# A new order for the first loads and early work, and one product moved between two attention bursts

## The chip, the cores and the metric

The kernel runs on one core of a Trainium2 chip. The metric is the device time of one execution in microseconds (us), the median of the runs. Five queues of instructions run beside one another and meet only at semaphores: TensorE (PE: matmuls, with the weight loads shown apart as PEld), VectorE (DVE), ScalarE (ACT), GpSimd (POOL) and SyncE (SP, which here issues nearly all DMAs).

## The reference

Four layers with residual connections on a sequence of S = 2048 tokens of width D = 448 in bf16: local attention (A), a gated feed-forward (B), A again and B again. Both attention layers use the same weights, and so do both feed-forward layers.

```python
def _A_ref(x, wqkv, wo):                 # H = 16 heads of 28, W, dil = 8, 2
    qkv = (x @ wqkv).reshape(B, S, 3, H, Dh)        # q, k, v by head
    # token t sees the keys t, t-2, ..., t-14
    logits = einsum("bhsd,bhswd->bhsw", q, kg) * Dh ** -0.5
    attn = softmax(where(mask, logits, -1e9))
    return einsum("bhsw,bhswd->bhsd", attn, vg).reshape(B, S, D) @ wo

def _B_ref(x, w_gate, w_up, w_down):     # F = 1792
    return ((x @ w_gate) * (x @ w_up)) @ w_down

x = x + _A_ref(_layernorm(x), A_wqkv, A_wo)
x = x + _B_ref(_layernorm(x), B_w_gate, B_w_up, B_w_down)
x = x + _A_ref(_layernorm(x), A_wqkv, A_wo)
x = x + _B_ref(_layernorm(x), B_w_gate, B_w_up, B_w_down)
```

## The kernel before

x stays in SBUF as 16 blocks of 128 tokens. In the code the layers are numbered 0 to 3; 0 and 2 are attention, so "the second layer" of attention is layer 2. The attention layers are cut into chunks of tokens: layer 0 into 256, 512, 512, 512 and 256, that is blocks 0-1, 2-5, 6-9, 10-13 and 14-15.

Work is first described as some 1580 numbered operations, each with the engines it may run on and what it depends on. No planner decides on the order: the table `ORDER` (line 103) lists by hand, for each of the five engines, the numbers of its operations in the order of execution, and so also says which of ACT and DVE makes a copy that either could make. The table `BANKS` (line 164) gives for each operation of PE that opens accumulators the PSUM banks (of eight) that it takes. A bank must have been read by its last user before it is taken again; `schedule` (line 223) derives that wait from the two tables, and `emit` (line 273) writes the instructions and semaphore waits out. An instruction at the head of an engine's queue that waits holds up all that stand behind it.

The head of the kernel, up to about 50 us, is what most of the change touches:

- SP issues the loads of x (line 443, called from `load_x`, line 448) in six pieces: operation 0 is block 0, 1 is block 1, 2 is blocks 2-3, 7 is blocks 4-7, 12 is blocks 8-11, 13 is blocks 12-15. Operations 3 to 6 load four pieces of the Q/K weight into a staging area (3 is piece 1, 4 is piece 3, 5 is piece 0, 6 is piece 2), 8 and 9 the V weight, 72 to 83 the gate and up weights, 84 to 87 the output weight `wo_g`, 71 writes constant rows of ones to a scratch tensor in DRAM that V passes through later.
- Layer norm of a block: DVE takes statistics (lines 571 and 573), ACT turns the variance into 1/std with two small functions (574, 576), DVE normalises into `xn_sb` (592). PE transposes the block (602 for the first two blocks, 606 for others), and ACT or DVE copies the result into `xnTa` (613, 616).
- ACT and DVE copy the staged Q/K weight into its padded form `WQK`, in eight pieces (line 510); later DVE adds small extra columns (518).
- PE makes V of a group of query blocks (`v_group`, copies at 766 to 793) and Q and K of a chunk (`qk_chunk`): four groups of fourteen matmuls each, 256 or 512 columns wide. All ordinary matmuls come from one helper and have line 351. A pair of matmuls on the two halves of the array's rows runs side by side. ACT or DVE copies a group to `qk` (701).
- Attention of a group of query blocks: DVE makes two masked copies of Q (`Qz`, 812), PE the scores (S, line 826), ACT the exponential (835), DVE the mask (842), PE the product with V (AV, line 860: 64 small matmuls in a burst), ACT and DVE copy it to `O_sb` (871, 875), and a normalisation follows (DVE 885, ACT 886 and 887, DVE 898). The output projection (`y_blocks`, PE line 351 with `wo_g`) adds to x at 915.

A large product is "crossed": its two accumulators are each fed from both halves of the rows, first one way, then the other. The second half of the work waits for the first (line 639), and each half may itself be two operations. For the down projection of a feed-forward chunk (`twin_blocks`, line 656, called with line 977) that makes four operations of fourteen matmuls: 1240, 1241, 1242 and 1243 for blocks 4 and 5 in layer 3, each 448 columns wide. Operation 1233 is to blocks 2 and 3 what 1241 is to 4 and 5.

In the second attention layer PE has 1308, the AV burst of group 6, directly followed by 1330, the AV burst of group 7, and then 1241. Elsewhere in PE's list an entry such as `1303*1.3.5/1223` mixes a burst into another operation's matmuls.

Of the kernel before, what the change touches and what calls it, by code (L numbers as in the profile page):

```python
# [95 lines left out]
def grp_nc(g):  # L96
# [35 lines left out]
    ),  # L132
    "dve": (
# [46 lines left out]
)  # L180


class Op:
    __slots__ = ("engs", "ins", "est", "deps", "mode", "prio", "acquire", "release", "idx", "eng",
                 "dma", "after", "selfd", "alt")

    def __init__(self, **kw):
        for k in self.__slots__:
            setattr(self, k, kw.get(k))
# [907 lines left out]
```

## Time and profile before

| | us |
|---|---|
| median of 3 runs | 383.92 (383.89 to 384.61) |
| the profiled execution | 384.08 |
| its span, first to last instruction | 382.3 |
| PE busy | 376.2 |
| DVE busy | 286.4 |
| ACT busy | 205.1 |

In the rows below, a line of the timeline reads: start, duration, engine, source line, operation, the tile written and the tiles read, shape, how many instructions were merged into the row, and in brackets the idle time in front and what ended it. A line of the waits reads: who waited for whom, us in total, times, and the longest. "issue" stands for waiting that nothing in the profile explains. In the chain, a row has its start, duration and what ran. The granted clock (PEclk) is in tenths of full speed, cut off at 9.

### The profile page before, as it was taken

What the parts mean: (1) busy time and instruction counts of PE and PEld (TensorE: products, weight loads), DVE (VectorE), ACT (ScalarE), POOL (GpSimd) and SP (SyncE); (2) the same over time, 40 slices, a digit from 0 to 9 for tenths busy, and PEclk for the clock granted to TensorE, in tenths of its full rate; (3) what the DMA queues carried; (4) which work ended last, traced back from release to release, by engine and by line L of the source; (5) the groups of instructions that cost most, each with busy time, mean ns of one, the idle gap of its engine ahead of it and who ended that gap; (6) DMA issues with size and microseconds to landing.
All of it is one profiled execution on the core that took longest, in us unless ns stands there. A gap on an engine that the chain in (4) does not pass through costs nothing.

```text
span 382.3 us, 14251 instructions
## 1 busy us (share of the span) xinstructions
PE 376.2 (98%) x6322; PEld 210.1 (55%) x6322; DVE 286.4 (75%) x643; ACT 205.1 (54%) x390; POOL 5.0 (1%) x25
## 2 busy tenths in 40 slices
PE   8999999999999999999999999999999999999997
PEld 3545587544445445444756765545555444446664
DVE  7987999998976786787677985637998698455323
ACT  4999886756426552564465525547744635133320
POOL 5000000000000000000000000000000000000000
PEclk9999999999999999999999999999999999999999
DMA  7756633610611033031101135320125004140003
GB/s 241 195 139 174 91 90 102 84 23 2 89 35 38 2 60 62 15 67 26 32 14 33 20 43 101 39 45 4 27 34 74 3 2 68 32 115 30 3 2 98
DMA packets 54881, 22.50 MB, mean 59 GB/s; under 512 B 45012, under 2 KB 54820, under 8 KB 54820
## 3 DMA queue, kind: packets, MB, share of 16 engines
q1 hardware_dynamic: 54676, 21.53, 27.8%
q8 instruction: 50, 0.82, 0.9%
q14 instruction: 11, 0.09, 0.1%
q10 hardware_dynamic: 144, 0.06, 0.1%
HBM read 8.54 MB, written 2.71 MB: 29 GB/s over the span
## 4 chain that ended last, share of the span: by engine, by line
PE 92%; ACT 2%; DVE 2%; DMA 1%; SPq 1%; issue 1%; DVEq 0%
PE ps L351 83%; PE ps L354 3%; PE ps L860 2%; PE ps L826 2%; PE ps L966 1%; DMA hT<-in_A_wqkv_dram 1%; ACT qk L701 1%; SPq L443 1%; ACT E_sb L835 1%; DVE xn_sb L592 0%; PE ps L606 0%; ACT xnTa L616 0%; DVE Qz L812 0%; DVE R_sb L885 0%; ACT lnv L574 0%
## 5 line engine op out<-in xcount | busy, mean ns | idle before, releaser
L351 PE MATMUL ps<-xnTb,WGU 64*128 64x512 bf16 (+1 forms) x1894 | 172.4, 332 | 0.0
L351 PEld LDWEIGHTS ps<-xnTb,WGU 64*128 64x128 bf16 x1894 | 92.0, 94 | 69.8 <-issue 1.4
L951 ACT ACTIVATE g_sb<-ps 128x512 bf16<-128x512 f32 (+1 forms) x140 | 70.1, 510 | 85.0 <-PE ps L351 65.2
L954 DVE TENSOR_TENSOR hT<-g_sb,ps 128x512 bf16<-128x512 bf16 (+1 forms) x140 | 78.2, 575 | 47.0 <-ACT g_sb L951 44.5
L351 PE MATMUL ps<-WD,hT 64*128 64x448 bf16 x812 | 82.8, 350 | 0.0
L351 PEld LDWEIGHTS ps<-WD,hT 64*128 64x128 bf16 x812 | 38.8, 94 | 34.8 <-DVE hT L954 0.3
L351 PE MATMUL ps<-xnTa,WQK 64*128 64x512 bf16 (+1 forms) x494 | 53.3, 353 | 0.3 <-DVE WQK L518 0.2
L915 DVE TENSOR_TENSOR x_sb<-x_sb,ps 128x448 bf16<-128x448 bf16 x62 | 37.2, 613 | 15.6 <-PE ps L351 15.3
L835 ACT ACTIVATE E_sb<-ps,shift_sb 128x1024 bf16<-128x1024 f32 (+1 forms) x36 | 37.1, 1068 | 12.7 <-PE ps L826 12.5
L571 DVE BATCH_NORM_STATS2 st<-x_sb 128x6 f32<-128x448 bf16 x64 | 38.8, 616 | 1.6 <-DMA x_sb<-in_A_x_dram 1.1
L592 DVE TENSOR_SCALAR xn_sb<-x_sb,mv,rstd 128x512 bf16<-128x512 bf16 (+1 forms) x64 | 35.4, 567 | 5.5 <-ACT rstd L576 5.5
L351 PEld LDWEIGHTS ps<-xnTa,WQK 64*128 64x128 bf16 x494 | 23.2, 94 | 21.5 <-ACT E_sb L835 0.5
L701 ACT ACTIVATE qk<-ps 128x1024 bf16<-128x1024 f32 (+1 forms) x29 | 27.0, 950 | 14.3 <-PE ps L351 14.2
L351 PE MATMUL ps<-wo_g,oT 64*128 64x448 bf16 x250 | 28.7, 350 | 0.0
L842 DVE TENSOR_TENSOR E_sb<-E_sb,MK 128x1024 bf16<-128x1024 bf16 (+1 forms) x36 | 23.3, 659 | 5.3 <-ACT E_sb L835 5.2
L886 ACT ACTIVATE R_sb<-R_sb 128x480 f32<-128x480 f32 (+1 forms) x34 | 20.3, 602 | 10.8 <-DVE R_sb L885 10.8
L898 DVE TENSOR_TENSOR oT<-O_sb,R_sb 128x480 bf16<-128x480 f32 (+3 forms) x36 | 22.1, 624 | 4.3 <-ACT R_sb L887 4.2
L351 PE MATMUL ps<-WV,xnTa 64*128 64x336 bf16 (+3 forms) x252 | 24.0, 305 | 0.1
L885 DVE STREAM_SHUFFLE R_sb<-O_sb 128x480 f32<-128x480 f32 (+1 forms) x34 | 23.1, 694 | 0.0
L574 ACT ACTIVATE lnv<-mv,eps_sb 128x2 f32<-128x2 f32 (+1 forms) x33 | 9.4, 294 | 22.3 <-DVE mv L573 22.2
L887 ACT ACTIVATE R_sb<-R_sb 128x480 f32<-128x480 f32 (+1 forms) x34 | 20.2, 602 | 0.6
L871 ACT ACTIVATE O_sb<-ps 128x512 f32<-128x512 f32 (+3 forms) x19 | 10.3, 557 | 14.1 <-PE ps L860 14.1
(60 smaller groups left out, 214.1 us busy)
## 6 DMA issues: line engine op xcount, KB each, us to landing
out_dram<-x_sb SPq DMA_DIRECT2D x15, 112.0 KB, 1.8
x_sb<-in_A_x_dram SPq DMA_DIRECT2D x3, 448.0 KB, 6.6
hT<-in_A_wqkv_dram SPq DMA_DIRECT2D x4, 224.0 KB, 5.1
WGU<-in_B_w_gate_dram SPq DMA_DIRECT2D x4, 224.0 KB, 3.5
WGU<-in_B_w_up_dram SPq DMA_DIRECT2D x4, 224.0 KB, 3.5
WD<-in_B_w_down_dram SPq DMA_DIRECT2D x2, 448.0 KB, 3.8
WGU<-in_B_w_gate_dram SPq DMA_DIRECT2D x2, 336.0 KB, 4.7
WGU<-in_B_w_up_dram SPq DMA_DIRECT2D x2, 336.0 KB, 4.9
```

The lines of the kernel that those rows point to most:

```text
L351: return lambda E: E.matmul(out(), lhs(), rhs(), start=start, stop=stop)
L571: sc.add("dve", one(lambda E, B=B: E.bn_stats(st6[:, B, :], x_sb[:, B, :]), ("bn", li, B)), 525.0, deps=[("x", li - 1, B)] + ([("xn", li - ...
L592: sc.add("dve", one(lambda E, B=B, dst=dst, src=src: E.tensor_scalar(dst, src, mv[:, B, 0:1], rstd[:, B:B + 1], ALU.subtract, ALU.mult), ( ...
L701: return E.activation(dst, src, ACT.Copy) if hasattr(E, "activation") else E.tensor_copy(dst, src)
L835: return E.activation(E_sb[:, slot, 2 * hp:2 * hp + 2, 0:w], ps[:, b0:b0 + 2, 0:w], ACT.Exp, bias=shift_sb[:, 0:1], scale=SCALE)
L842: return E.tensor_tensor(e, e, MK[:, kind, 0:nc].unsqueeze(1).unsqueeze(1).to_broadcast([128, 2, w // nc, nc]), ALU.min)
L885: sc.add("dve", one(lambda E: E.stream_shuffle(R_sb[:, rs, 0:w], O_sb[:, os_, 0:w], [DH] * 32), ("Rs", li, qb)), dve_est(w) + 20.0, deps=[ ...
L886: sc.add("act", one(lambda E: E.activation(R_sb[:, rs, 0:w], R_sb[:, rs, 0:w], ACT.Ln), ("Rl", li, qb)), act_est(w, False), deps=[("Rs", l ...
L898: return E.tensor_tensor(oT[:, :, a % HALF:a % HALF + z - a], O[:, :, a - tok:z - tok], R_sb[:, rs, 0:w].rearrange("p (h n) -> p h n", h=4 ...
L915: sc.add("dve", one(lambda E: E.tensor_tensor(x_sb[:, B, :], x_sb[:, B, :], ps[:, bk[w], 0:D], ALU.add), ("x", li, B)), dve_est(D), deps=[ ...
L951: sc.add("act", one(lambda E, gs=gs, bk=bk: E.activation(g_sb[:, gs, 0:nt], ps[:, bk[0], 0:nt], ACT.Copy), ("G", li, j, fc)), act_est(nt), ...
L954: sc.add("dve", one(lambda E, gs=gs, bk=bk, fc=fc: E.tensor_tensor(hT[:, fc, hs, 0:nt], g_sb[:, gs, 0:nt], ps[:, bk[1], 0:nt], ALU.mult), ...
```

## The change

Only the two tables change. The numbers of the operations, what each does and what each depends on stay as they are. The words that came with the change give the order of the first x loads as 1, 0, 2-3, 4-7; SP's list in the diff has 0, 1, 2-3, 4-7, where it was 1, 2-3, 0, 4-7.

SP, early part: the order of the x loads and of the four Q/K weight pieces, the constant rows (71) behind the output weight, 83 ahead of 82, and 85 last of its four.

```diff
-        "1 2 0 7 8 9 6 3 4 5 13 72 12 74 73 10 11 71 75 76 77 78 79 80 81 85 86 84 87 82 83 89 291 293 ...
+        "0 1 2 7 8 9 5 4 6 3 13 72 12 74 73 10 11 75 76 77 78 79 80 81 86 84 87 85 71 83 82 89 291 293 ...
```

PE, early part: the transposes of blocks 0 and 1 (101, 104) ahead of four warming matmuls (55 to 58), that of block 3 (122) ahead of the first full V product (232), those of blocks 5, 6, 7, 12 and 15 (128, 143, 146, 173, 188) and some halves of Q/K products moved by a few places.

```diff
-        "41 42 ... 53 54 55 104 56 101 57 58 119 202 203 232 128 125 233 196 192 122 197 193 220 226 221 227 222 143 146 223 194 190 "
-        "195 191 224 149 152 225 207 346 185 170 347 241 344 212 345 342 176 167 343 173 246 236 490 237 488 491 188 489 492 567 ...
+        "41 42 ... 53 54 101 104 55 56 57 58 202 119 203 122 232 125 233 128 192 196 193 197 220 226 221 146 222 227 223 194 143 190 "
+        "195 191 224 149 152 225 207 346 185 170 347 241 344 212 345 342 176 167 343 246 236 173 237 490 488 188 491 489 492 567 ...
```

PE, late: operation 1241 between the two bursts.

```diff
-        "1233 1240 1308 1330 1241 1297 1242 1234 1298 1243 1235 1397 1394 1388 1400 ...
+        "1233 1240 1308 1241 1330 1297 1242 1234 1298 1243 1235 1397 1394 1388 1400 ...
```

ACT and DVE, early part (up to about 38 us; the rest of both lists is unchanged). Block 0's statistics come before block 1's, those of blocks 5 and 4 (114, 112) before the normalisation of block 2 (118), and that of block 3 (121) directly behind it. Copies that change engine: of the Q/K weight 59 (DVE to ACT) and 61 (ACT to DVE); of transposes 144 (block 6, ACT to DVE), 174 and 189 (blocks 12 and 15, DVE to ACT); 239 (a V copy) and 248 (an O copy) from ACT to DVE. 262, the masked Q of group 2, moves from before the normalisations to behind them.

```diff
 act
-        "14 98 99 94 95 110 111 102 105 116 117 61 65 204 129 205 126 123 201 234 199 235 134 135 228 231 140 144 141 147 229 200 182 158 183 153 159 164 230 "
-        "208 165 209 186 352 243 242 351 177 350 248 217 218 238 239 251 252 255 256 497 498 572 ...
+        "14 94 95 98 99 110 102 111 105 116 59 117 204 65 123 205 126 129 234 199 134 135 201 235 228 147 140 231 141 229 182 200 164 158 183 159 165 153 230 "
+        "209 208 186 352 243 242 351 177 350 174 217 238 218 251 252 189 255 497 256 498 572 ...
 dve
-        "15 17 16 96 97 108 92 109 93 106 103 107 100 112 118 114 113 115 120 63 62 127 124 66 64 60 59 121 132 130 160 ...
-        ... 210 166 175 213 214 215 245 244 168 216 174 247 "
-        "249 262 187 250 219 254 189 253 496 257 261 260 286 ...
+        "16 15 17 92 96 93 97 106 108 100 109 103 107 114 112 115 118 113 121 60 120 66 124 127 64 63 61 62 132 130 178 ...
+        ... 175 166 210 214 213 215 245 244 216 172 168 247 248 "
+        "249 250 187 219 254 239 253 496 257 262 261 260 286 ...
```

The bank table gives the head other banks for single operations. From operation 494 on, and for most before it, it is the old table with the banks renamed in whole pairs: 01 to 67, 23 to 01, 67 to 23, 45 as it was.

```diff
-        "41:0 101:2 104:1 119:45 122:45 125:45 128:01 143:23 146:45 149:67 152:01 ...
+        "41:0 101:1 104:2 119:67 122:01 125:67 128:01 143:67 146:67 149:23 152:01 ...
...
-        "1297:01 1303:2367 1308:01 1320:47 1325:0123 1330:23 ...
+        "1297:67 1303:0123 1308:67 1320:43 1325:6701 1330:01 ...
```

66 rows, old and new, of tables (BANKS, ORDER) are left out of this document.

## The prediction

> **What bounds the kernel now.** I read the page first, then the list of waits, then the chain.
>
> ```profile
> span 382.3 us, 14251 instructions
> PE 376.2 (98%) x6322; PEld 210.1 (55%) x6322; DVE 286.4 (75%) x643; ACT 205.1 (54%) x390; POOL 5.0 (1%) x25
> PEclk9999999999999999999999999999999999999999
> q8 instruction: 50, 0.82, 0.9%
> PE 92%; ACT 2%; DVE 2%; DMA 1%; SPq 1%; issue 1%; DVEq 0%
> ```
>
> PE is busy for 98% of the span at the full granted clock, and 92% of the chain is PE. The change removes no matmul, so it can only take away PE's pauses: all idle time is 382.3 - 376.2 = 6.1 us. Some lie before the first data and behind the last product, and no line of the diff touches those. Two remain in reach: the head up to about 50 us, and one pause late in the kernel, which the list of waits names as the only one of PE after 287 us.
>
> ```profile
> PE ps L860 <- issue: 0.5, 1, 0.5
> PE ps L826 <- DVE qk L701: 0.5, 1, 0.5
> PEld ps L606 <- DVE xn_sb L592: 2.0, 4, 0.9
> PE ps L606 <- ACT E_sb L835: 0.2, 1, 0.2
> PE ps L351 <- DVE WQK L518: 0.2, 1, 0.2
> ```
>
> "issue" means that no semaphore explains the pause; the other rows are of the head, where PE waits for DVE and ACT.
>
> **The late move: fourteen matmuls between two groups.** Line 860 is the attention product (AV); the 448-wide L351 product with WD is the down projection. PE's rows around the pause, a lone AV burst elsewhere, and two short bursts in a row elsewhere, all from the timeline:
>
> ```profile
> 284.98 1.38 PE L860 MATMUL ps<-E_sb,v_sb 64*32 64x64 bf16 x125
> 286.86 0.21 PE L860 MATMUL ps<-E_sb,v_sb 64*32 64x64 bf16 x3 [0.50 <-issue]
> 287.00 1.50 PE L351 MATMUL ps<-WD,hT 64*128 64x448 bf16 x14
> ...
> 41.90 0.81 PE L351 MATMUL ps<-xnTa,WQK 64*128 64x512 bf16 x6
> 42.64 0.68 PE L860 MATMUL ps<-E_sb,v_sb 64*32 64x64 bf16 x64
> 43.26 1.04 PE L351 MATMUL ps<-xnTa,WQK 64*128 64x512 bf16 x8
> ...
> 200.64 0.68 PE L860 MATMUL ps<-E_sb,v_sb 64*32 64x64 bf16 x64
> 201.23 0.74 PE L826 MATMUL ps<-Qz,qk 64*32 64x64 bf16 x64
> 201.90 0.55 PE L351 MATMUL ps<-WD,hT 64*128 64x448 bf16 x4
> ...
> q8 instruction: 1, 0.02, 45.1%
> ...
> 23.43 0.86 PE ps L351 x8
> ```
>
> The q8 row is the DMA view of 284.0 to 284.2 us: one packet on the instruction queue. The last is from the chain: eight 512-wide matmuls in full flow. The page counts 50 such packets, and PE has 2 x 6322 = 12,644 matmuls and weight loads: about one packet for 253 of them. From 284.98 PE ran 125 matmuls and their loads, 250 instructions, in 1.4 us, then stood for 0.50 us and went on in the middle of a burst. I read it as PE having used up its fetched block before the next, asked for at 284.0, was there. The pair at 200.64 to 201.90 is as dense and has no pause, so density alone doesn't do it; a packet must be under way.
>
> Price: today the two bursts take 287.00 - 284.98 = 2.02 us. The diff puts the first fourteen-matmul half of the down projection's crossing (op 1241) between them. A lone burst lasts 43.26 - 42.64 = 0.62. Entering it costs something: six 512-wide matmuls in full flow take 0.86 x 6/8 = 0.64, but 42.64 - 41.90 = 0.74, so 0.10. Two separate bursts with one further entry are 0.62 + 0.10 + 0.62 = 1.34, and the saving 2.02 - 1.34 = 0.68. It holds only if the block is there in time: PE resumed at 286.86, and with the fourteen matmuls ahead (1.50 by their row, the last 0.2 of it overlapped) it reaches that spot at 284.98 + 0.62 + 1.3 + 0.10 + about 0.4 = 287.4, later than 286.86. Bounds: a gain of 0.68, and a loss of 0.10 if the pause merely moves. I take 0.68.
>
> [...]
>
> What is queued behind it: the second burst now ends near 287.6 instead of 287.0. ACT's first copy of it waits there already, and two normalisations queue behind that copy:
>
> ```profile
> 287.11 0.60 ACT L871 ACTIVATE O_sb<-ps 128x512 f32<-128x512 f32 x1 [2.87 <-PE ps L860]
> 289.21 0.60 ACT L886 ACTIVATE R_sb<-R_sb 128x480 f32<-128x480 f32 x1 [0.62 <-DVE R_sb L885]
> 292.21 0.86 DVE L793 CAST v_sb<-ps 128x672 bf16<-128x672 f32 x1 [0.50 <-PE ps L351]
> ```
>
> ACT stood 0.62 us before 289.21, waiting for DVE, whose work there hangs on the first burst alone; so a copy 0.6 late is absorbed, and DVE's V copy at 292.21 waits for PE and comes earlier with it. No PE wait follows to the end, so the 0.68 reaches the end. Op 1241 reads the same gated products as op 1233, its counterpart for the two blocks before, which stands ahead of both bursts already: it won't wait.
>
> **The head.** The diff's SP list loads x block 0, then 1, 2-3, 4-7 (the words of the change say 1, 0; the list decides), and the four weight pieces as 0, 3, 2, 1. Same transfers, same sizes; each issue keeps its cost. Rows of the first 13 us:
>
> ```profile
> 6.84 0.63 DVE L571 BATCH_NORM_STATS2 st<-x_sb 128x6 f32<-128x448 bf16 x1 [0.35 <-DMA x_sb<-in_A_x_dram]
> 7.38 0.40 DVE L592 TENSOR_SCALAR xn_sb<-x_sb,mv,rstd 128x512 bf16<-128x512 bf16 x1
> 10.16 0.83 DVE L510 COPY WQK<-hT 128x448 bf16<-128x448 bf16 x4
> 10.90 0.41 DVE L592 TENSOR_SCALAR xn_sb<-x_sb,mv,rstd 128x512 bf16<-128x512 bf16 x1
> 11.27 0.83 PE L351 MATMUL ps<-xnTa,WQK 64*128 64x256 bf16 x12
> 12.48 0.60 ACT L616 ACTIVATE xnTa<-ps 128x512 bf16<-128x512 bf16 x1 [0.47 <-PE ps L606]
> ```
>
> 1. Blocks 0 and 1 swap and both are done early; the four warming matmuls behind them only fill PE. Nothing.
> 2. DVE now takes the statistics of blocks 5 and 4 (loaded at 6.84) before the normalisation of block 2 at 7.38: that comes at 6.84 + 0.63 + 0.62 = 8.1, 0.7 late, and delays the first full V product by some 0.4. But the Q/K products of chunk 0 wait for the last weight copy, which ends at 10.16 + 0.83 = 11.0 (same copies, same four transfers) and start at 11.27 either way. What hides the 0.4 is this wait.
> 3. Block 3 is normalised at 10.90 today, so its transposed copy ends at 12.48 + 0.60 = 13.08, and chunk 1's 512-wide products start only then. In the new order it follows block 2 at once, at about 8.5. Two of chunk 0's groups, 28 matmuls, run through; twelve take 0.83 with a last 0.2 that overlaps, so 0.054 each: 11.2 + 1.5 = 12.7. Gain 13.1 - 12.7 = 0.4.
> 4. From there to 28 us the order is shuffled but the products are the same and PE's pauses small (0.2 and 0.2 in the waits above, both behind copies that follow PE). Copies change engine: the transposes of blocks 12 and 15 go from DVE to ACT, one V copy and one O copy from ACT to DVE. About 0.35 of the 0.4 should arrive at 28 us.
> 5. There the gain meets a chain on DVE. The first output projection (L351 with wo_g) waits for the third normalisation (L898 at 35.47).
>
> ```profile
> 29.48 0.67 DVE L871 COPY O_sb<-ps 128x512 f32<-128x512 f32 x1
> 30.38 0.84 DVE L812 TENSOR_SCALAR Qz<-qk,qmask 128x960 bf16<-128x960 bf16 x2
> 33.36 0.41 DVE L616 COPY xnTa<-ps 128x512 bf16<-128x512 bf16 x1
> 35.47 0.65 DVE L898 TENSOR_TENSOR oT<-O_sb,R_sb 128x480 bf16<-128x480 f32 x1
> 38.49 1.15 DVE L915 TENSOR_TENSOR x_sb<-x_sb,ps 128x448 bf16<-128x448 bf16 x2 [2.37 <-PE ps L351]
> ...
> 29.59 0.55 ACT L871 ACTIVATE O_sb<-ps 128x448 f32<-128x448 f32 x1
> 31.87 0.73 ACT L793 ACTIVATE v_sb<-ps 128x672 bf16<-128x672 f32 x1
> ...
> 36.34 0.92 PE L351 MATMUL ps<-wo_g,oT 64*128 64x448 bf16 x8
> ```
>
> DVE is full from 29.48 to 35.47 + 0.65 = 36.12, and the projection starts 0.2 behind. The new list takes out the masked Q copies (0.84, into the idle 2.37 before 38.49) and one transpose copy (0.41), and puts in the O copy (about 0.65, as on DVE at 29.48) and the V copy (0.86 by the row at 292.21): 0.26 more. Block 12's transposition moves behind the second AV burst, so the chain starts some 0.5 earlier, not 0.35. Then 36.12 - 0.5 + 0.26 = 35.9; about 0.2 more goes where it waits for ACT, which now has two transpose copies of 0.60 ahead of the normalisations. That is 36.1 against PE's own arrival of 36.0: the projection starts at 36.15 instead of 36.34. I take 0.2. Bounds: a gain of 0.4 if DVE keeps up, a loss of 0.7 if both copies (0.55 + 0.73 on ACT's rows, less the 0.5) land on the chain.
> 6. SP: the constant rows for V (128 KB) go from 16.64 to behind the wo loads; their first reader is far behind, at 51.31. The last two weight pieces are issued up to 0.86 later than at 33.09, for products after 49.66. SP waits there for transfers anyway. Nothing.
>
> ```profile
> 16.64 0.86 SPq L443 DMA_DIRECT2D vt<-ones  x1
> 51.31 1.14 SPq L721 DMA_TRANSPOSE v_sb<-vt  x1
> ```
>
> From operation 494 on the bank numbers are renamed in whole pairs, so who waits for whom is unchanged there: nothing.
>
> **The sum.** -0.68 - 0.2 = -0.88, say -0.9 us. The profiled execution took 384.08, of which 382.3 is the span; it stands 0.16 above the median of 383.92. From the median: 383.0. What can be told from no change is 0.2%, 0.77 us.
>
> **Rivals.** (a) The late pause is no fetch and goes with the second burst. For: the view names no releaser; against: the pause in mid-burst and the packet at 284.0. Then +0.10 - 0.2: 383.8. [...] (b) Slower: the copies that changed engine put both ACT's and DVE's additions on the chain to the projection at 36.34. Price: 1.28 on DVE and 1.2 on ACT (two of 0.60), up to 2.5 if nothing overlaps, less 0.68: to 385.7. It decides against the change once the projection starts 0.7 later than 36.34, and measurably at 1.5. Against it: DVE loses 0.84 + 0.41 there as well. (c) The head gives its full 0.4: 382.8. (d) The head loses up to 0.7 and the late move pays: 383.2 to 383.9.
>
> **How the numbers follow.** My forecast with (c), both places faster: 0.60, of which 0.51 beyond 0.2%. (a) 0.15, (d) 0.13, both within 0.2%; (b) 0.12, of which 0.09 beyond. So faster 0.51, same 0.40, slower 0.09. The likeliest case alone spans 382.7 to 383.3. The range, 382.6 to 384.1, takes in (a), (d) and the small end of (b).
>
> **What would show it.** Right: no "issue" row on PE at L860, two bursts of 64 with fourteen 448-wide matmuls between; the first 512-wide Q/K product before 13; the first wo_g product near 36.15; every later stage earlier by the head's gain alone up to 285, and 0.68 more behind. Wrong: an "issue" pause elsewhere, the wo_g product later than 36.34, or a new PE wait in the head.

## The result and the profile after

The changed kernel takes 383.42 us (median, 382.5 to 384.33), the kernel before, run beside it on the same chip, 384.46. The ratio is 0.9977 with a 95% interval of 0.9967 to 0.9986, or -0.88 us of 384.46 (between -1.27 and -0.54). (By the two medians it is -1.04.) The prediction had 383.0 from 383.92, a ratio of 0.9976.

The profiled execution is the fastest of its runs, 382.5 with a span of 380.8; the one before took 384.08 with a span of 382.3. So the two profiles are 1.58 apart where the medians are 1.04 apart, and about 0.5 us of what they show is the scatter of single executions. Where that scatter arises is one of the findings below.

The page of the kernel after: the span, the busy times and the chain that ended last.

```profile
span 380.8 us, 14251 instructions
PE 375.8 (99%) x6322; PEld 210.2 (55%) x6322; DVE 287.0 (75%) x644; ACT 203.6 (53%) x389; POOL 5.1 (1%) x25
PE 94%; DVE 2%; ACT 1%; issue 1%; DMA 1%; SPq 0%; DVEq 0%
```

PE is busy for 375.8 against 376.2, with the same 6322 matmuls: the work is the same, and the kernel is bound by PE as before. PE's timeline around the two bursts, after (start, duration, what ran):

```profile
284.08 0.68 PE L860 MATMUL ps<-E_sb,v_sb 64*32 64x64 bf16 x64
284.69 1.50 PE L351 MATMUL ps<-WD,hT 64*128 64x448 bf16 x14
286.12 0.68 PE L860 MATMUL ps<-E_sb,v_sb 64*32 64x64 bf16 x64
286.74 0.60 PE L351 MATMUL ps<-WV,xnTa 64*128 64x336 bf16 x6
```

Two bursts of 64 with fourteen matmuls of 1241 between, no bracket with an idle time, each burst 0.61 to 0.62 from its start to that of the next row. The pause of 0.50 is gone, and no wait of PE follows up to the end. The same view of the head:

```profile
7.49 0.36 PE L351 MATMUL ps<-WV,xnTa 64*128 64x224 bf16 x3
9.80 0.73 PE L351 MATMUL ps<-WV,xnTa 64*128 64x448 bf16 x6
10.48 3.85 PE L351 MATMUL ps<-xnTa,WQK 64*128 64x256 bf16 x48
35.37 0.92 PE L351 MATMUL ps<-wo_g,oT 64*128 64x448 bf16 x8
```

The first Q/K product starts at 10.48 (11.27 before), the first output projection at 35.37 (36.34 before). What lay between 0 and 284 gained 0.90 (the first burst starts at 284.08 against 284.98), what lay behind it 0.69. The head gave four to five times what the prediction had put on it.

The traffic points to a cause. Busy times by stretches: the stretch and its length, then what PE, PEld, DVE, ACT and POOL were busy with the number of instructions, the granted clock, the busy share of the DMA engines, and last the GB/s. The kernel before, then the kernel after:

```profile
4.00:6.00 2.00, 1.98 (x9) 0.69 (x7) 2.00 (x6) 0.80 (x4) 1.54 (x7) 1.00 0.88 254
6.00:8.00 2.00, 1.43 (x19) 0.84 (x19) 1.65 (x6) 1.47 (x4) 0.50 (x2) 1.00 1.03 359
8.00:10.00 2.00, 1.71 (x30) 0.81 (x25) 1.70 (x8) 1.28 (x5) 0.00 (x0) 1.00 1.04 376
```

```profile
4.00:6.00 2.00, 2.00 (x11) 0.74 (x9) 1.81 (x7) 0.89 (x4) 1.54 (x7) 1.00 1.04 338
```

Between 4 and 6 us the changed kernel loads at 338 GB/s, the old one at 254. By the events on the semaphore that SP's load of blocks 4-7 raises, these have landed at 6.14 against 6.81, and the last of the four weight pieces at 9.80 against 10.46. The prediction had called them the same transfers at the same cost. Whether the order of the first three loads does this, or the new list behind it, or one lucky execution, is what experiments 5 to 7 and the second profiles ask.

### The profile page after: what moved, and what is told of

The parts are those of the page before. It is cut to its first block, busy times and chain, and to the rows that moved or that the text cites. A ratio compares the mean times of both kernels' runs of the same rounds, so it can differ in the third digit from the quotient of the medians.

```text
span 380.8 us, 14251 instructions
## 1 busy us (share of the span) xinstructions
PE 375.8 (99%) x6322; PEld 210.2 (55%) x6322; DVE 287.0 (75%) x644; ACT 203.6 (53%) x389; POOL 5.1 (1%) x25
## 4 chain that ended last, share of the span: by engine, by line
PE 94%; DVE 2%; ACT 1%; issue 1%; DMA 1%; SPq 0%; DVEq 0%
PE ps L351 85%; PE ps L354 3%; PE ps L860 2%; PE ps L826 2%; PE ps L966 1%; ACT E_sb L835 1%; DMA x_sb<-in_A_x_dram 1%; DVE xn_sb L592 1%; DVE st L571 0%; PE ps L606 0%; DVE Qz L812 0%; DVE R_sb L885 0%; DVE E_sb L842 0%; SPq L443 0%; DVE qk L701 0%
```

## The experiments

Two questions. **Late move:** is the pause a fetch that depends on how many instructions PE has behind it (the theory), or does it belong to a second burst that follows the first directly (rival a)? **Head:** does the gain come from the reordered work (steps 3 to 5 of the prediction) or from the order of the loads, which the prediction had put at nothing? Medians are in us; "before" is the kernel before, timed beside them on the same chip: 384.28 for the first four, 384.58 for the next three, 384.33 for the last four.

**1. The late move alone.** The kernel before, with one edit:

```diff
-"1233 1240 1308 1330 1241 1297 ...
+"1233 1240 1308 1241 1330 1297 ...
```

> The kernel before with the late move alone (operation 1241 between the two AV bursts). Theory F (the pause is an instruction block that came late): no pause on PE at L860; from the first AV matmul to the first product behind the second burst, without the fourteen matmuls between, 1.34 us instead of 2.02; time 0.68 us less than before, ratio 0.9982. Rival P (the pause belongs to the second burst and goes with it): a pause of 0.5 us in the second burst, ratio 1.000 to 1.0003. The head is that of before either way.

Measured: 384.06, ratio 0.9989 (0.9979 to 0.9999), or -0.42 us, between -0.81 and -0.04. PE's timeline of this kernel:

```profile
286.10 0.68 PE L860 MATMUL ps<-E_sb,v_sb 64*32 64x64 bf16 x64
286.71 1.50 PE L351 MATMUL ps<-WD,hT 64*128 64x448 bf16 x14
288.14 0.74 PE L860 MATMUL ps<-E_sb,v_sb 64*32 64x64 bf16 x64
```

The pause goes with this edit alone, and PE waits for nothing from there to the end. The first product behind the second burst starts at 288.81; without the fourteen matmuls (1.43 from start to start) the two bursts take 1.28, where 1.34 was expected and the kernel before has 2.02.

**2. The head alone.** The changed kernel with the late edit undone (`1308 1330 1241`).

> The changed kernel with the late move taken back. Theory: the head's new order is worth 0.2 to 0.4 us (ratio 0.9990 to 0.9995), and the pause of 0.5 us at L860 is back. Rival: the 0.95 us by which the changed kernel's profiled execution was ahead at 49 us all comes from the order, ratio 0.9975. What decides is when the loads land: if the fourth x load (blocks 4-7) lands near 6.8 us, as before, the order alone is seen; if it lands near 6.1 again, the order of the loads makes them faster.

Measured: 383.70, ratio 0.9977 (0.9968 to 0.9987), or -0.88 us. The pause is back, in the same place:

```profile
284.64 1.33 PE L860 MATMUL ps<-E_sb,v_sb 64*32 64x64 bf16 x124
286.46 0.21 PE L860 MATMUL ps<-E_sb,v_sb 64*32 64x64 bf16 x4 [0.49 <-issue]
286.60 1.50 PE L351 MATMUL ps<-WD,hT 64*128 64x448 bf16 x14
```

So the head alone yields about as much as the whole change. The prediction had given it 0.2.

**3. The bursts left together, the product ahead of both.** The kernel before with

```diff
-"1233 1240 1308 1330 1241 1297 ...
+"1233 1240 1241 1308 1330 1297 ...
```

> The kernel before with operation 1241 ahead of both AV bursts, which still follow one another. Theory F: the fourteen matmuls give the block 1.3 us more to arrive before the bursts reach its end (2.34 us after it was asked for today, 2.84 needed), so no pause; time 0.6 to 0.7 us less, ratio 0.9983. Rival P (two AV bursts in a row stall by themselves): the pause of 0.5 us stays, ratio 1.000.

Measured: 384.88, ratio 1.0013 (1.0004 to 1.0021). PE's timeline of this kernel:

```profile
286.72 1.36 PE L860 MATMUL ps<-E_sb,v_sb 64*32 64x64 bf16 x128
289.02 0.60 PE L351 MATMUL ps<-WV,xnTa 64*128 64x336 bf16 x6 [0.94 <-DVE O_sb L875]
```

The two bursts are adjacent and run through, 128 in one row. So, in this execution, a burst that follows directly doesn't stop, and rival (a) loses its mechanism. But nothing stands between the second burst and the V product 1297 any more, which needs a bank that DVE reads first: 0.94 of waiting takes the place of the pause, 0.50 in the profile before. Fourteen matmuls between the bursts thus do two things: the pause is gone and this wait is covered.

**4. Only the number of instructions ahead changed.** The kernel before, with the first nine warming matmuls (which compute nothing that is used) cut into eight pieces of 64 columns: 63 more matmuls and as many weight loads on PE, all in the first 7 us: 126 instructions more, so that whatever goes by their count comes 126 instructions earlier in the work.

```diff
-matmul(ps[:, bank, :], warm[:, 0:128], warm)                     # shortened
+for a in range(0, 512, 64): matmul(ps[:, bank, a:a + 64], warm[:, 0:128], warm[:, a:a + 64])
```

> [...] Theory F: the block's end moves from the 61st matmul of the second burst to the end of the first, and is asked for among slow 448-wide products several us earlier; the pause at L860 is gone or under 0.2 us although the two bursts still follow one another; another may appear where a block now ends in a dense burst. Time 0.3 to 0.7 us less, ratio 0.9983 to 0.9992, if the head isn't disturbed. Rival P: the pause of 0.5 us stays where it is, ratio 1.000.

Measured: 384.99, ratio 1.0018 (1.0007 to 1.0028). PE's timeline of this kernel, with the bursts adjacent and their surroundings untouched:

```profile
286.85 1.51 PE L862 MATMUL ps<-E_sb,v_sb 64*32 64x64 bf16 x128
288.29 1.50 PE L351 MATMUL ps<-WD,hT 64*128 64x448 bf16 x14
```

Nothing near the bursts was changed, only the count of instructions in front of them, and they run through. The pause has moved: the timeline of PEld, the weight loads of the same kernel, has one of 0.54 that the profile can't explain at 206 us, where the profile before has none.

```profile
206.28 0.10 PEld L351 LDWEIGHTS ps<-WD,hT 64*128 64x128 bf16 x2 [0.54 <-issue]
```

There the matmuls are 448 wide, and PE loses about half of it: against the profile before, it falls behind by 0.29 between 201 and 206 us. Another 0.27 is lost between 72 and 89, and it begins with a second such wait of the weight loads, again where the profile before has none:

```profile
75.54 0.11 PEld L351 LDWEIGHTS ps<-WV,xnTa 64*128 64x128 bf16 x3 [0.31 <-issue]
```

The traces allow a count. Take the recorded instructions of PE (matmuls, weight loads and the few others) in order of start. In all five profiles that have the pause in the bursts, it stands behind exactly 10,433 of them; in experiment 2, where PE has two more of the others recorded, one matmul fewer of the bursts runs before it. The two waits of this kernel stand behind 7,360 and 3,008. The differences are 10,433 - 7,360 = 3,073 = 12 x 256 + 1 and 7,360 - 3,008 = 4,352 = 17 x 256 (records can be missing: of the 63 added matmuls 62 are there). No larger step fits both to within one. So 256 instructions is an estimate of the step, from these three counts, and the prediction had counted one packet on the instruction queue for 253 of them. A data dependence would not move with the count in such steps. That it is a fetch, in blocks of about that many, is the author's inference, from the packet beside the pause in the profile before and from this; what these profiles show is that it goes by the count, and that it cost less among wide matmuls (0.29 of a wait of 0.54). The profiled execution is later mainly for another reason: its head was 1.4 us later than in the profile before (operation 300, one of the first gate and up products, at 51.02 instead of 49.65).

**5. The order of the first three loads alone.** The kernel before; no work is reordered.

```diff
-"1 2 0 7 8 9 6 3 4 5 13 ...
+"0 1 2 7 8 9 6 3 4 5 13 ...
```

> The kernel before with one edit: SP issues x block 0 ahead of blocks 1 and 2-3; everything else, the weight pieces too, as before. Theory O (the order of the first three x loads decides how fast the next transfers land): the load of blocks 4-7 lands near 6.1 us as in the two profiles with the new list (6.14 both), not at 6.8 to 7.7 as in the four with the old one, and the DMA rate from 4 to 6 us is near 335 GB/s, not 195 to 254; all later loads 0.7 us or more earlier, time 0.5 to 0.9 us less (ratio 0.9977 to 0.9987). Rival V (the landing depends on something else: the compute queues, or chance): 6.8 to 7.7, ratio 0.9995 to 1.001, since block 1's statistics then come 0.4 later.

Measured: 383.69, ratio 0.9979 (0.9968 to 0.9989), or -0.81 us: as much as the head as a whole. Traffic of this kernel:

```profile
4.00:6.00 2.00, 2.00 (x6) 0.68 (x5) 1.66 (x6) 0.60 (x3) 1.54 (x7) 1.00 1.02 323
```

The difference lies in little more than one microsecond, from 3.5 to 4.75 us. The kernel before, then this one:

```profile
3.50:4.75 1.25, 1.25 (x7) 0.47 (x6) 1.10 (x4) 0.50 (x2) 0.95 (x4) 1.00 0.56 121
```

```profile
3.50:4.75 1.25, 1.25 (x5) 0.42 (x4) 0.87 (x3) 0.50 (x2) 0.95 (x4) 1.00 1.04 320
```

So the earlier loads are shown, and the shorter time is shown. How the one becomes the other is seen only in part: in this profile the first 512-wide Q/K product starts at 13.32, against 13.14 and 13.67 in the two profiles of the kernel before. The profiled execution, 384.07, is a late one for this kernel; its warming matmuls stayed slow until 6.9 us, and the first transposes, at 7.29, stood behind them.

**6. The whole new SP list under the old work, and 7. the old SP list under the new work.** The diff of both is the SP list as shown in the change, in the one direction and the other.

> The kernel before with all of the new SP list and nothing else of the change. Theory O: blocks 4-7 land near 6.1 us. The old order of DVE then waits for weight piece 1, which the new list loads last (near 9.8 instead of 9.3 to 10.2), so less of it is kept than in the run with the x loads alone: time 0.2 to 0.7 us less, ratio 0.998 to 0.9995. Rival V: landing at 6.8 to 7.7, time 0.3 to 1.0 us more than before because of that wait.

> The changed kernel with SP's old list. Theory O: blocks 4-7 land at 6.8 to 7.7 us again. DVE's new order has a copy of weight piece 0, now loaded last (10.5 to 11.7), ahead of block 2's transposed copy, so the first full V product starts near 11 instead of 8.8 and the time is 0.5 to 1.5 us above the changed kernel's, near before or above: ratio 1.000 to 1.003. Rival V: landing near 6.1 although the list is the old one, since the compute queues are those of the changed kernel.

Measured: the new list under the old work 384.76, ratio 1.0012 (0.9996 to 1.0028); the old list under the new work 385.26, ratio 1.0025 (1.0008 to 1.0043). DVE's timeline of the first, and PE's behind it:

```profile
9.43 0.28 DVE L510 COPY WQK<-hT 128x448 bf16<-128x448 bf16 x1 [0.50 <-DMA hT<-in_A_wqkv_dram]
10.01 0.28 DVE L510 COPY WQK<-hT 128x448 bf16<-128x448 bf16 x1 [0.30 <-DMA hT<-in_A_wqkv_dram]
10.66 0.61 PE L606 MATMUL ps<-ident,xn_sb 64*128 64x64 bf16 x16 [0.71 <-DVE xn_sb L592]
```

And of the second:

```profile
10.51 0.28 DVE L510 COPY WQK<-hT 128x448 bf16<-128x448 bf16 x1 [1.43 <-DMA hT<-in_A_wqkv_dram]
11.27 0.74 PE L351 MATMUL ps<-WV,xnTa 64*128 64x448 bf16 x6 [1.63 <-ACT rstd L576]
```

In both DVE stands at a weight copy whose piece lands late, because list and work want the pieces in different orders. In the first the normalisation queued behind the copy holds PE for 0.71. In the second ACT stands at a weight copy as well, for 1.40; what is queued behind the two copies, the transposed copy of block 2 on DVE and a small function of the layer norm on ACT (the one that the row names), holds PE for 1.63. Loads by the new list land early in the first (blocks 4-7 at 6.08) and it doesn't help; the new order of the work without its loads is slower than the kernel before, although it has the late move. The order of the weight pieces and that of the work have to be changed together.

**8. The kernel before once more**, for a second profile of it.

> The kernel before once more, for the profile alone. Theory O: blocks 4-7 land at 6.8 us or later and the rate from 4 to 6 us is 195 to 255 GB/s, as in the four profiles with the old list so far. Chance alone would put it near 6.1 in some executions of the old list too.

Measured: 384.51; blocks 4-7 land at 7.36, traffic between 4 and 6 us is 269 GB/s. The pause is there but shorter, with 125 matmuls before it and three behind:

```profile
285.69 1.38 PE L860 MATMUL ps<-E_sb,v_sb 64*32 64x64 bf16 x125
287.29 0.21 PE L860 MATMUL ps<-E_sb,v_sb 64*32 64x64 bf16 x3 [0.23 <-issue]
```

**9. The three loads and the late move, nothing else.** The edits of 1 and 5 together.

> The kernel before with two edits only: the first three loads of x in the order 0, 1, 2-3, and operation 1241 between the two bursts. No compute in the head is reordered. If the order of three loads and the late move are all that counts, the two ratios found singly multiply, 0.9979 x 0.9989 = 0.9968 (a median some 1.2 us below before), as fast as the whole change or faster. If the reordered head work carries a share, as my steps 3 to 5 had it (0.2 us), this stays about 0.2 us behind the whole change. Trace: the last piece of x (blocks 4-7) lands near 6.1 us, the first 512-wide Q/K product stays near 13.3, no pause in the late burst.

Measured: 383.35, ratio 0.9974 (0.9965 to 0.9983), or -1.00 us.

**10. The changed kernel once more.**

> The changed kernel once more. Its head alone gave 0.9977 and the late move alone 0.9989. If the two add, the whole change gives 0.9966; by its first timing it gave 0.9977. Expected in between, 0.9965 to 0.9980. Trace: the first full V product at 7.5 us if the warming matmuls speed up near 4.5 us as in the first profile, at 8.1 if only near 6; the late burst some 276.6 us behind that product either way.

Measured: 383.25, ratio 0.9979 (0.9961 to 0.9997). So two swaps, of one load and of one product, are worth as much as the change as a whole, and what the reordered work of the head adds can't be told from nothing in the times. The profiled execution took 383.91. Traffic of this kernel, and PE's first rows:

```profile
4.00:6.00 2.00, 2.00 (x7) 0.65 (x5) 1.89 (x8) 0.89 (x4) 1.58 (x7) 1.00 1.02 301
```

```profile
1.28 5.74 PE L502 MATMUL ps<-hT 128*128 128x512 bf16 x14 [1.28 <-DVE hT L473]
6.85 0.61 PE L602 MATMUL ps<-ident,xn_sb 128*128 128x128 bf16 x8
8.52 0.46 PE L351 MATMUL ps<-WV,xnTa 64*128 64x224 bf16 x6 [0.19 <-DMA WV<-in_A_wqkv_dram]
```

The same rows in the first profile of the same program:

```profile
1.28 4.74 PE L502 MATMUL ps<-hT 128*128 128x512 bf16 x14 [1.28 <-DVE hT L473]
5.91 0.79 PE L602 MATMUL ps<-ident,xn_sb 128*128 128x128 bf16 x8
```

Fourteen warming matmuls take 4.74 in one execution and 5.74 in the other. Block 0 is normalised by 5.9 in both (its row on DVE starts at 5.45 and at 5.48 and takes 0.40). In the first the transposes start then; in the second they stand behind the warming matmuls until 6.85, and the V weight is late as well. The first V product is at 8.52 instead of 7.49. The last Q/K weight piece lands at 11.15 instead of 9.80, and the first Q/K product is at 11.78 instead of 10.48; operation 300 is at 50.06 instead of 48.70: 1.36 of the 1.41 us between the two executions (382.5 and 383.91) are there before 50 us. Late matmuls and late loads come together in this pair, and it doesn't tell their shares apart.

**11. The warming matmuls shortened.** The changed kernel with the three warming matmuls ahead of the first transposes cut to 64 columns.

```diff
-matmul(ps[:, bank, :], warm[:, 0:128], warm)                     # shortened
+matmul(ps[:, bank, 0:w], warm[:, 0:128], warm[:, 0:w])     # w = 64 for n in (11, 12, 13), else 512
```

> The changed kernel with the last three warming matmuls ahead of the first transposes cut from 512 columns to 64 (they compute nothing that is used). If it is true that the transposes of blocks 0 and 1 wait for the warming matmuls whenever these speed up late (0.6 us in the profile of the head alone, 0.05 in that of the whole change), the first transpose now starts at 5.9 us in either case, and the median comes 0 to 0.6 us below that of the changed kernel. If the later speed-up itself, not the queue, is what costs, or if the shorter warming delays the speed-up, nothing is gained or up to 0.5 us lost.

Measured: 382.81 (382.69 to 383.02), ratio 0.9964 (0.9952 to 0.9976). PE's timeline of this kernel:

```profile
1.28 5.04 PE L502 MATMUL ps<-hT 128*128 128x512 bf16 x14 [1.28 <-DVE hT L473]
6.12 0.91 PE L602 MATMUL ps<-ident,xn_sb 128*128 128x128 bf16 x8
7.83 0.46 PE L351 MATMUL ps<-WV,xnTa 64*128 64x224 bf16 x6
```

PE was still slow at 5.95, as in the second profile of the changed kernel, and yet the transposes start at 6.12, 0.73 earlier than there, and the first V product 0.69 earlier. So they did stand behind the warming matmuls. (The loads were early in this execution, the last Q/K weight piece at 9.71, so what follows later isn't due to the edit alone.) 6.12 is 0.2 later than expected: the eleven long ones end at 5.95, behind the normalisation. The median is 0.44 below that of the changed kernel beside it, but the intervals of the two ratios overlap: a likely improvement, not one that these runs establish.

**12. Only the three loads back in the old order**, in the changed kernel (`1 2 0 7` for `0 1 2 7`).

> The changed kernel with only the first three loads of x back in the old order (1, 2-3, 0); the new order of the weight pieces and of all work stays. If the order of the three loads decides how soon the later ones land, blocks 4-7 land at 6.5 to 7.7 us again instead of 6.1, the first full V product comes 0.5 us or more later, and the time rises by 0.7 to 1.0 us, to about the kernel before. If the order matters only because the new order of work wants block 0 first, block 0 alone is late and blocks 4-7 land near 6.1 all the same.

Measured: 383.96, ratio 1.0004 (0.9980 to 1.0027; one of the ten executions took 388.53), 0.71 above the changed kernel by the medians. All ten executions lie above the changed kernel's median, though the intervals of the two ratios overlap. Blocks 4-7 land at 6.71. Traffic of this kernel:

```profile
4.00:6.00 2.00, 2.00 (x7) 0.65 (x5) 1.80 (x5) 0.49 (x3) 1.56 (x7) 1.00 0.91 232
```

That is the undoing of experiment 5 from the other end, and the loads slow down again: from 3.5 to 4.75 us they run at 157 GB/s, against 312 and 303 in the two profiles of the changed kernel.

**All profiles side by side.** Loads: when blocks 4-7 have landed (by the events on their semaphore), and GB/s between 4 and 6 us. Then starts of the first matmul of some operations, in PE's order: 220 is the first 512-wide Q/K product, 258 the first output projection, 300 one of the first gate and up products, at the end of the head; "burst" is 1308, "to end" the time from it to the last matmul.

| kernel | x order | blocks 4-7 | GB/s | 220 | 258 | 258 - 220 | 300 | burst | to end |
|---|---|---|---|---|---|---|---|---|---|
| before | old | 6.81 | 254 | 13.14 | 36.34 | 23.20 | 49.65 | 284.98 | 94.72 |
| before, again | old | 7.36 | 269 | 13.67 | 36.91 | 23.24 | 50.32 | 285.68 | 94.44 |
| 1 late move | old | 7.72 | 197 | 14.10 | 37.33 | 23.23 | 50.72 | 286.10 | 94.09 |
| 3 ahead of both | old | 6.99 | 204 | 13.42 | 36.66 | 23.24 | 50.08 | 286.71 | 93.68 |
| 12 after, old loads | old | 6.71 | 232 | 13.08 | 36.40 | 23.32 | 49.72 | 285.06 | 94.03 |
| 7 after, old SP list | old | 6.50 | 255 | 14.48 | 37.80 | 23.32 | 51.12 | 286.43 | 94.03 |
| 4 warming cut | old | 7.42 | 195 | 13.78 | 37.70 | 23.92 | 51.02 | 286.85 | 94.14 |
| 5 three loads | new | 6.00 | 323 | 13.32 | 36.52 | 23.20 | 49.84 | 285.23 | 94.44 |
| 9 loads and late | new | 6.04 | 326 | 13.22 | 36.42 | 23.20 | 49.84 | 285.18 | 94.03 |
| 6 new SP list | new | 6.08 | 328 | 13.70 | 36.91 | 23.21 | 50.24 | 285.56 | 94.44 |
| 2 head alone | new | 6.14 | 336 | 12.63 | 35.98 | 23.35 | 49.29 | 284.64 | 94.66 |
| after | new | 6.14 | 338 | 12.02 | 35.37 | 23.35 | 48.70 | 284.08 | 94.03 |
| after, again | new | 6.34 | 301 | 13.30 | 36.72 | 23.42 | 50.06 | 285.48 | 94.03 |
| 11 warming short | new | 6.03 | 338 | 12.35 | 35.70 | 23.35 | 49.05 | 284.38 | 94.03 |

Three readings. The seven kernels with the old order of loads land blocks 4-7 at 6.50 to 7.72, the seven with the new one at 6.00 to 6.34; the rates are 195 to 269 and 301 to 338. Neither overlaps. Between 3.5 and 4.75 us the gap is wider still: 121 to 197 against 293 to 320. Experiments 5 to 8 ran on another chip than the other eight, and the split is the same on each. From operation 300 to the burst it is always 235.3 to 235.4 (aside from experiment 3, with fourteen more matmuls ahead of its burst, and experiment 4, with the pause in this stretch): whatever the head gains or loses arrives in full. And the time from the burst to the end is 94.03 to 94.14 wherever the late move or a shifted count took the pause away, and 94.44 to 94.72 where it stands (experiment 3, with fourteen matmuls fewer behind the start of its burst, is left out).

## Why the prediction was right, and where it was not

**The sum** was right: -0.9 forecast, -0.88 by the ratio, which from the prediction's 383.92 gives 383.04, inside the likeliest case's own 382.7 to 383.3. The measured median, 383.42, stands a little above that, because the kernel before was at 384.46 beside it; it is inside the range of 382.6 to 384.1. That the sum came out so near was luck: two terms erred in opposite directions, the late move with -0.68 where -0.42 was measured, the head with -0.2 where -0.88 was.

**The late move, -0.68.** Every sign that it named came: no "issue" row on PE, two bursts of 64, ACT's late copy absorbed, no PE wait behind. The profiled pair gives 94.72 - 94.03 = 0.69. But the size was taken from one execution with a long pause: in five profiles that have it, it was 0.50, 0.49, 0.23, 0.22 and 0.22, and the move then gives 94.44 - 94.03 = 0.41. By time it is -0.42, between -0.81 and -0.04. The term should have been about -0.5. Rival (a) fell with experiments 3 and 4 and the count in steps of 256. The profile before has 50 packets on the instruction queue and one such pause of PE. That one, 0.22 to 0.50 us in the five profiles on the engine that bounds the kernel, is what the move took away.

**The head, step 2.** This is the step that failed: "same copies, same four transfers", with the Q/K products "at 11.27 either way". The transfers were the same, but their times were not. The order of the first three loads, costed at nothing, is worth -0.81 by time (experiment 5) and blocks 4-7 land some 1.0 us earlier with it (7.07 and 6.11, the means of the table). In the profile after, the weight copies on DVE ended at 9.46 + 0.83 = 10.29 instead of 11.0, and the first Q/K product came at 10.48. The rows show no idle time of PE in front of this product in either profile, so the copies are not all that it stood behind; the V products ahead of it were earlier too.

```profile
9.46 0.83 DVE L510 COPY WQK<-hT 128x448 bf16<-128x448 bf16 x4
```

The bounds of the head, +0.7 to -0.4, had no such term, and -0.88 lies outside them. A row that would have warned stood in the profile before: 254 GB/s between 4 and 6 us against 359 and 376 in the two stretches behind it. The loads were not at the rate that they reached later, so their order could matter.

**Step 1** (blocks 0 and 1, nothing) missed what the order of transposes and warming matmuls does: when the warming matmuls stay slow, the transposes stand behind them, 0.97 us in one profile (normalised by 5.88, transposed at 6.85).

**Step 3, a gain of 0.4 at the first 512-wide product.** With loads in the new order, this product starts at 13.32 and 13.22 under the old work (experiment 6 aside, where the order of the weight pieces doesn't fit the work) and at 12.02, 12.63 and 13.30 under the new. The means are 0.6 apart, but the scatter is 1.3. The sign "before 13" held in two of three. **Step 5** held: between that product and the first projection the new work takes 23.32 to 23.42, the old 23.20 to 23.24 (experiment 4 is left out, where another delay falls in this stretch), so the chain on DVE takes back about 0.15; forecast was 0.15 to 0.2. (The step's bound of a loss, 0.55 + 0.73 less 0.5, is 0.78 and not 0.7.) So steps 3 to 5 describe what is in the trace, but in the times their sum is not to be seen (experiments 9 and 10), and with the old loads the new work brings nothing beyond the late move, which experiment 12 has (383.96 against 384.33), or a loss (7). **The order of the four Q/K weight pieces**, put at nothing with the loads, does matter: experiments 6 and 7 show waits of 0.80 and 1.43 on DVE when list and work disagree. In the change they agree. **Step 6**, the constant rows and the last gate and up pieces, at nothing: its moves touch products from about 50 us on, and the even 235.3 to 235.4 behind operation 300 shows no cost or gain there.

**Rival (b)** did not come: the projection starts at 35.37, not 0.7 later than 36.34. **(c)** was too small: the head gave more than its full 0.4. **(d)** did not come with the new loads; with the whole old SP list under the new work the head lost more than (d) allowed, with the projection at 37.80, 1.46 later than before.

**What stays open:** why the order 0, 1, 2-3 lets the transfers behind it run faster. It is shown that it does, in seven profiles against seven, and where: between 3.5 and 4.75 us. What holds them back there in the old order was not tried. How much of the -0.81 goes through the earlier loads isn't shown either: the profiles of experiments 5 and 9 have the loads early and the first 512-wide product at 13.32 and 13.22, no earlier than the 13.14 of the profile before. Nor is it settled what the reordered work of the head is worth by itself. The singly measured parts, -0.88 and -0.42, sum to more than the whole of -0.88; their uncertainties of some 0.4 each leave room for that.

## What to carry to other kernels

Where a kernel waits for its first loads, their order can be a term of its own (-0.81 us here): look at the traffic in the first microseconds, and if it is below the rate reached later (here 254 against 359 and 376 GB/s), give it bounds of its own, of both signs. Before a small pause is costed from one profile, see how it varies from one execution to the next; here it halved (0.50 and 0.23 in two profiles of the kernel before), and the start of the first V product moved by 1.03 us between two profiles of the kernel after (7.49 and 8.52). Change the order of loads and of the work that eats them together, and test each alone, since half a change was slower than none here (ratio 1.0025 for the new work with the old SP list).

## What the runs showed of the hardware

- **The rate of the loads depends on their order** (195 to 269 against 301 to 338 GB/s between 4 and 6 us, 121 to 197 against 293 to 320 between 3.5 and 4.75; the same transfers on the same queue, seven profiles each).
- **The warming matmuls speed up at different times.** A 512-wide warming matmul starts 0.43 us behind the one before, later 0.21. By the starts of the single matmuls the switch fell near 4.0 us in the profile before, 4.4 in that after, 5.5 in experiment 6, 6.9 in experiment 5 and 7.2 in experiment 3, which is 2.7 to 5.9 us after PE's first matmul. Two rows show it, fifteen matmuls each, the kernel before and the one of experiment 5:

```profile
1.25 4.73 PE L502 MATMUL ps<-hT 128*128 128x512 bf16 x15 [1.25 <-DVE hT L473]
```

```profile
1.25 6.20 PE L502 MATMUL ps<-hT 128*128 128x512 bf16 x15 [1.25 <-DVE hT L473]
```

  The granted clock is given as 1.00 in these stretches all the same. The spread of the switch is 3.2 us, with 7 slow matmuls in the profile before and 14 in experiment 3; what sets it was not shown. In experiment 10 this switch (4.4 and 6.5 us) and the later loads (the last Q/K weight piece at 9.80 and 11.15) differ between two executions of the same program, and 1.36 of the 1.41 us between them arise there, before 50 us.
- **A pause on PE of 0.22 to 0.50 us depends on the number of instructions ahead of it**, and turns up elsewhere, as waits of the weight loads of 0.54 and 0.31, when 126 are added in the first 7 us: 3,073 and 7,425 instructions before its old place, 12 and 29 times 256 to within one. Among 448-wide matmuls the wait of 0.54 cost PE 0.29.
